# The last feed-forward item of a spectral block: its products in another order, the last comparisons earlier

## The chip, the cores and the metric

One Trainium2 chip, one of its cores. The metric is the device time of one execution in microseconds (us); of several executions the median counts. A profile is one further execution, recorded with every instruction's begin and end.

## The reference

`x` has 2048 rows of 512. It goes through a Fourier mixing of rows and columns and then through a gated feed-forward block of inner width 1792; both sit behind a normalization with a learned shift, scale and gate.

```python
x = A_x
mod = (_silu(c) @ w_mod).reshape(c.shape[0], 6, 1, -1)
sa, ca, ga, sb, cb, gb = (mod[:, 0], mod[:, 1], mod[:, 2], mod[:, 3], mod[:, 4], mod[:, 5])
h = _layernorm(x, axis=-1) * (1 + ca) + sa
x = x + ga * _A_ref(h, A_dft_seq_re, A_dft_seq_im, A_dft_hid_re, A_dft_hid_im)
h = _layernorm(x, axis=-1) * (1 + cb) + sb
x = x + gb * _B_ref(h, B_w1, B_w3, B_w2)
```

`_A_ref` multiplies by the real and imaginary DFT matrices that are given as inputs. `_B_ref` is `(silu(h @ w1) * (h @ w3)) @ w2`.

## The kernel before, in words

`folded` computes the Fourier part with about half of the products, since DFT matrices are symmetric. Whether the given matrices are so, it finds out itself: it loads them a second time in pieces (tiles `cx`, `cy`, `cz`, `cv`; `cx` and `cz` by queue SP, `cy` and `cv` row by row by POOL) and compares the pieces on DVE, counting differences in `cnt`. `judge` (L1759) sums the counts in a chain of some twenty small DVE instructions down to one flag, `bad`. Behind the last store every engine loads the flag, and if it is set, the program goes on with `general`, a second version without the shortcut. The comparisons are a queue of work beside the products: `to_load` holds loads, `checks` holds comparisons, and `look` (L2649), called after each unit of products, starts loads while more than `spare()` of the 50 SBUF slots are free, and starts a comparison once its tiles were begun `LAG` = 9 units ago.

The feed-forward block runs over 14 items: 2 pairs of row blocks (a pair is two blocks of 512 rows) by 7 groups of 256 inner columns. Each item is made of units of six matmuls of 128x512 (two contraction halves by three passes, since every factor is split into a high and a low part of fp32):

- a1 to a7 are the products with `w1`, b1 to b7 those with `w3`. Seven products give what eight would, in the way of Winograd: the four results (two halves of the group's columns by two row blocks) are sums of products. The products 1, 6, 7, 4 add up in one PSUM bank (bank 0 for a, 3 for b), 2 has a bank of its own (1 or 4), and 5 and 3 share one (2 or 5). Between them `factor` (L2100) takes partial sums out: ACT copies (`x`, `y`), DVE adds (`plus`).
- A result of a goes through SiLU on ACT; the matching result of b is multiplied to it on DVE; then the high part of the product is made on ACT and the low part on DVE (both in a tile `hf`). `behind(n, ...)` puts a step behind the n-th following unit.
- Of the four results, two belong to the first row block: they need the products 1, 2, 6, 7, 4. The two of the second row block need 5 and 3 too.
- y units are the products of `hf` with `w2`. An item has eight: four blocks of 128 output columns for the first row block and four for the second. They are put into the queue `seconds` once the item's results are on the way, and run between the units of the next item. For the last two items a y unit's sum is multiplied by the gate and added to `xr` on DVE (L1890); the last item's are then stored by queues SP and ACT (L1861).

The order of units is written by hand as a string for each item (`head + body`, L2767 on); "-b7" is a unit of the item before, "y" the next of `seconds`, "J" runs what is left of the comparisons and then `judge`. In this text y1 to y8 are the eight y units of the last but one item, and z1 to z8 those of the last item (z1 to z4 for its first row block).

The y units take PSUM banks 6 and 7 in turn. In the last item, once all seven a products are issued, the list becomes five banks long:

```python
if not more and kind == "a" and state[i, "w1"]["n"] == 7:
    down_banks[:] = [6, 7, 0, 1, 2]
```

A unit of the same list place waits until the sum that was there has been read.

Of the kernel before, what the change touches and what calls it, by code (L numbers as in the profile page):

```python
# [43 lines left out]
def folded(nc, pools, c, cp, wmr, wmc, x, xt, ctr, cti, wdr, wdi, w1, w3, w2, out):  # L44
# [42 lines left out]
    def copy(dst, src, scale=1.0):  # L87
        nc.scalar.activation(dst, src, AF.Copy, scale=scale)  # L88
# [1549 lines left out]
    to_load = deque()  # L1638
# [278 lines left out]
    def weight_jobs(i, w):  # L1917
        key = (w, *items[i])
        use = wuse[key] = {}

        def highs():
            use["h"] = take(F32R, w + "h")
            copy(flat(use["h"]), flat(wraw[key]))

        def totals(engine="DVE"):
            use["s"] = take(F32, w + "s")
            s, r = four(use["s"]), four(wraw[key])
            tensors(engine, s[:, 0, :], r[:, 2, :], r[:, 3, :], OP.add)
            tensors(engine, s[:, 1, :], s[:, 0, :], r[:, 0, :], OP.subtract)
            tensors(engine, s[:, 2, :], r[:, 0, :], r[:, 2, :], OP.subtract)  # L1930
            tensors(engine, s[:, 3, :], r[:, 1, :], s[:, 1, :], OP.subtract)

        def lows(engine="DVE"):
            use["l"] = take(F32R, w + "l")
            r = wraw.pop(key)
            tensors(engine, flat(use["l"]), flat(r), flat(use["h"]).bitcast(F32), OP.subtract)
            give(r)

        def sum_highs():
            use["sh"] = take(F32R, w + "sh")  # L1940
            copy(flat(use["sh"]), flat(use["s"]))

        def sum_lows(engine="DVE"):
            use["sl"] = take(F32R, w + "sl")
            tensors(engine, flat(use["sl"]), flat(use["s"]), flat(use["sh"]).bitcast(F32), OP.subtract)
            give(use.pop("s"))
            done.add(("ready", i, w))

        step(jobs, 1, highs, 0.0, 1.0)
        step(jobs, 1, totals, 1.4)  # L1950
        step(jobs, 1, lows, 1.2)
        step(jobs, 1, sum_highs, 0.0, 1.0)
        step(jobs, 1, sum_lows, 1.2)
# [145 lines left out]

    def factor(i, w, n):  # L2100
        g, pair = items[i]
        key = (w, g, pair)
        st = state.setdefault((i, w), {})
        new = n in (1, 2, 5)
        if new:
            st[TO[n]] = bank(TO[n] + (0 if w == "w1" else 3))
        to = st[TO[n]]
        names = ("h", "l") if LEFT[n][0] == "h" else ("sh", "sl")
        for d in range(2):
            at = slice(int(LEFT[n][1]) * HALF + d * P, int(LEFT[n][1]) * HALF + (d + 1) * P)  # L2110
            product(
                to,
                [flat(wuse[key][x])[:, at] for x in names],
                [x[:, d, :] for x in right(pair, n)],
                new and d == 0,
                d == 1,
                not new,
            )
        if n == 1:
            st["x"] = take(F32, "x")  # L2120
            if w == "w1":
                vs[i] = [take(F32, "v") for _ in range(2)]
        if n == 5:
            st["y"] = take(F32, "x")
        if n in (1, 5, 6):
            copy(st["y" if n == 5 else "x"][:, n // 6, :], to)
        elif n == 4:
            result(i, w, 1, 0, to)
        else:

            own = st["y" if n == 7 else "x"][:, n % 2 if n < 7 else 0, :]
            q, k = {2: (0, 0), 3: (0, 1), 7: (1, 1)}[n]
            dst = vs[i][q][:, k, :] if w == "w1" else own
            plus(dst, to, own)
            result(i, w, q, k, dst)
            if n == 7:
                behind(1, lambda: give(st["y"]))
        st["n"] = st.get("n", 0) + 1
        if st["n"] == 7:
            for x in wuse.pop(key).values():  # L2140
                give(x)
        if n == 3:
            behind(1, lambda: give(st["x"]))
            if w == "w3":
                for x in vs.pop(i):
                    behind(9 if items[i] in SEVEN else 3, lambda x=x: give(x))
# [494 lines left out]


    LAG, AHEAD, SPARE = 9, 7, 7
    clock, begun_at, paused = [0], {}, []

    def spare():
        return SPARE if ("xc", NT - 1) in done else SPARE + 2

    def look(force=False):  # L2649
        clock[0] += 1  # L2650
        while to_load and not paused and (len(free) > spare() or force) and len(begun_at) < AHEAD:
            key, fn = to_load.popleft()
            begun_at[key] = clock[0]
            fn()
        while checks:
            tiles, cost, fn = checks[0]
            late = any(x not in begun_at or clock[0] - begun_at[x] < LAG for x in tiles)
            if not force and (late or jobs or credit[0] <= 0):
                return
            if any(x not in begun_at for x in tiles):  # L2660
                return
            checks.popleft()
            credit[0] -= cost
            fn()
            for x in [x for x in begun_at if x not in cq]:
                begun_at.pop(x)
# [13 lines left out]
    turning = NG  # L2680
# [10 lines left out]
    def early_w3(i):  # L2691
        return items[i][1] == 1

    def unit(kind, i, n):
        g, pair = items[i]
        more = i + 1 < len(items)
        if n == 1:
            drain(lambda: ("ready", i, "w1" if kind == "a" else "w3") in done, jobs)
        if (kind, i, n) == ("a", turning, 1):
            drain(lambda: not background, background)  # L2700
        if kind == "a" and i == turning and n in (4, 5, 6, 7):
            drain(lambda: ("t", 1, {6: 2, 5: 1, 7: 3, 4: 4}[n]) in done, jobs)
        delayed()
        factor(i, "w1" if kind == "a" else "w3", n)
        if (kind, n) == ("a", 1):
            load_w(("w1", *items[i + 1]) if more else ("w2", g, pair))
        if (kind, n) == ("a", 6):
            load_w(("w2", g, pair))
        if not more and kind == "a" and state[i, "w1"]["n"] == 7:
            down_banks[:] = [6, 7, 0, 1, 2]  # L2710
        if (kind, n) == ("a", 7 if i == turning else 3) and more:
            load_w(("w3", *items[i + 1]))
            weight_jobs(i + 1, "w1")
        if (kind, n) == ("b", 2):
            (seven_jobs if (g, pair) in SEVEN else plain_jobs)(("w2", g, pair))
        if (kind, n) == ("b", 3):
            if i + 2 == turning:
                for at in ((PAIRS[1][0], 0), (PAIRS[1][0], 1), (PAIRS[1][1], 1)):
                    chunk_parts(background, *at, 3)
                sums_of.append(pair_sums(1))  # L2720
            if i + 1 == turning:
                other_operands()
            if more and not early_w3(i):
                weight_jobs(i + 1, "w3")
            if (g, pair) in SEVEN:
                seconds.extend((g, pair, n, ("w2", g, pair)) for n in ORDER7)
            else:
                for t in PAIRS[pair]:
                    seconds.extend((g, pair, t, d, ("w2", g, pair)) for d in range(ND))
        if (kind, n) == ("b", 6) and more and early_w3(i):  # L2730
            weight_jobs(i + 1, "w3")
        beside(1.36, FACTOR[kind][n])

    operand = {1: "h2l{0}.0", 2: "h2l{0}.1", 3: "h2l{1}.1", 5: "tl1", 6: "tl2", 7: "tl3", 4: "tl4"}
    prev = [f"all{b}.{m}" for b in (2, 3) for m in range(2)]
# [28 lines left out]
    for i in range(len(items)):  # L2764

        paused[:] = [i] if turning - 1 <= i < turning else []
        body = "a6 a5 y y a7 y a3 y a4 y b1 y b2 y b6 b5 y"  # L2767
        if i == turning:
            body = "y y y y y a6 y a5 y a7 y b1 b2 a4 b6 a3 b5"
        if i == len(items) - 1:  # L2770
            body = "a6 y a5 y b1 a7 y a3 b2 a4 y b6 b5 y b7 J y b4 b3 " + "y " * 10
        head = "-b7 a1 a2 -b4 -b3 "
        for what in (head + body).split() if i else []:
            if what == "J":
                while checks:
                    look(True)
                judge()
            elif what == "y":
                if not seconds:
                    continue  # L2780
                if (i, len(seconds)) == (len(items) - 1, 4):
                    tc.mark_branch_hint_location("general", hint="LikelyTaken")
                down(*seconds.popleft())
            elif what[0] == "-":
                unit(what[1], i - 1, int(what[2]))
            else:
                unit(what[0], i, int(what[1]))
# [806 lines left out]
```

## Time and profile before

| | |
|---|---|
| median of 3 runs | 638.33 us (637.39 to 640.04) |
| profiled execution | 641.07 us |
| its span, first to last instruction | 639.3 us |
| PE busy | 607.3 us, 95% of the span |
| DVE busy | 514.1 us, 80% |
| ACT busy | 391.0 us, 61% |
| POOL busy | 215.2 us, 34% |
| mean granted PE clock | 0.982 of full speed |

A row of the timeline gives start, busy time, engine, line, operation and tiles (out<-in) and, in brackets, how long the engine had been idle and who released it. Matmuls are pipelined: a row lasts 0.39 us, but the next starts 0.23 us after it. PEclk, the granted clock, is 1.00 where PE runs at full speed. Times count from the span's start.

### The profile page before, as it was taken

To read this page: it belongs to the slowest core of one execution; us is meant where nothing else is said; L and a number is where in the kernel's file an instruction comes from. 1 tells how busy PE (TensorE), PEld (TensorE's weight loads), DVE (VectorE), ACT (ScalarE), POOL (GpSimd) and SP (SyncE) were. 2 spreads that over 40 slices of the span, in tenths; PEclk is the share of its full clock that TensorE was granted. 3 is DMA by queue.
4 is the path that set the end of the run, shared out by engine and by line. 5 is a ranking of instruction groups with operands and counts; after the bars stand their busy time and mean duration, and the time that the engine had idled before them with its cause. 6 is when DMAs were issued, how large, how long until landed. Compare 5 with 4: busy or idle time off the path is not lost.

```text
span 639.3 us, 8734 instructions
## 1 busy us (share of the span) xinstructions
PE 607.3 (95%) x2893; PEld 491.5 (77%) x2893; DVE 514.1 (80%) x1017; ACT 391.0 (61%) x626; POOL 215.2 (34%) x234
## 2 busy tenths in 40 slices
PE   8998899999969999989999999899999999999984
PEld 3778889767747888868877888687878888888864
DVE  4997879889986998468947797699888979879883
ACT  2587787527665557976875666485656556665310
POOL 7344114483951022103023321510553344434000
PEclk9999999999969999999999999899999999999998
DMA  7762345798143398738679967999999999999406
GB/s 243 220 192 71 100 110 155 224 249 226 66 157 107 91 204 207 131 103 172 137 151 262 269 173 149 239 190 195 261 285 258 260 229 261 238 253 269 145 1 136
DMA packets 61585, 118.11 MB, mean 185 GB/s; under 512 B 10649, under 2 KB 29081, under 8 KB 61532
## 3 DMA queue, kind: packets, MB, share of 16 engines
q1 hardware_dynamic: 45068, 67.66, 38.3%
q0 software_dynamic: 13536, 46.93, 33.3%
q10 hardware_dynamic: 2928, 2.88, 1.6%
q8 instruction: 24, 0.39, 0.3%
q14 instruction: 29, 0.24, 0.1%
HBM read 84.94 MB, written 35.65 MB: 189 GB/s over the span
## 4 chain that ended last, share of the span: by engine, by line
PE 71%; DVE 11%; issue 8%; DMA 5%; ACT 3%; POOL 1%; DVEq 0%; ACTq 0%; POOLq 0%
PE banks L106 53%; PE banks L1295 4%; DMA sum<-y 3%; PE banks L929 3%; PE banks L1325 2%; DVE w3s L100 2%; PE banks L1474 2%; PE banks L599 1%; DMA wmr<-in_wmr 1%; PE banks L948 1%; PE banks L827 1%; PE banks L729 1%; DVE w1s L100 1%; DVE x L94 1%; DVE ml L100 1%
## 5 line engine op out<-in xcount | busy, mean ns | idle before, releaser
L106 PE MATMUL banks<-hf,w2h 128*128 128x512 f32 (+1 forms) x452 | 141.5, 393 | 6.2 <-DVE hf L91 3.1
L1899 POOL DMA_DIRECT2D sum<-y x48 | 44.7, 931 | 244.5 <-ACT y L656 206.4
L106 PEld LDWEIGHTS banks<-hf,w2h 128*128 128x128 f32 x452 | 84.9, 189 | 26.4 <-DVE hf L91 5.0
L106 PE MATMUL banks<-hf,w2l 128*128 128x512 f32 (+1 forms) x226 | 88.1, 390 | 0.0
L656 ACT ACTIVATE y<-banks,gb 128x512 f32<-128x512 f32 x96 | 65.5, 683 | 27.3 <-PE banks L106 24.0
L88 ACT ACTIVATE hf<-v 128x512 fp32r<-128x512 f32 x56 | 35.3, 631 | 62.4 <-DVE v L97 53.5
L94 DVE TENSOR_TENSOR x<-banks,x 128x512 f32<-128x512 f32 x42 | 28.9, 689 | 43.2 <-PE banks L106 40.4
L88 ACT ACTIVATE x<-banks 128x512 f32<-128x512 f32 x84 | 48.8, 591 | 18.2 <-PE banks L106 16.5
L1983 ACT ACTIVATE v<-v 128x512 f32<-128x512 f32 x42 | 26.5, 632 | 39.7 <-DVE v L94 38.9
L106 PEld LDWEIGHTS banks<-hf,w2l 128*128 128x128 f32 x226 | 42.9, 190 | 8.7
L94 DVE TENSOR_TENSOR v<-banks,x 128x512 f32<-128x512 f32 x42 | 28.9, 688 | 19.4 <-PE banks L106 19.0
L91 DVE TENSOR_TENSOR hf<-v,hf 128x512 fp32r<-128x512 f32 x56 | 38.4, 686 | 4.0 <-ACT hf L88 3.7
L106 PE MATMUL banks<-th,w3sh 128*128 128x512 f32 x84 | 33.2, 395 | 0.3 <-ACT x L88 0.3
L106 PE MATMUL banks<-th,w1sh 128*128 128x512 f32 x84 | 32.9, 392 | 0.0
L106 PE MATMUL banks<-tl,w1sh 128*128 128x512 f32 x84 | 32.8, 390 | 0.0
L106 PE MATMUL banks<-th,w3sl 128*128 128x512 f32 x84 | 32.7, 390 | 0.0
L106 PE MATMUL banks<-th,w1sl 128*128 128x512 f32 x84 | 32.7, 390 | 0.0
L106 PE MATMUL banks<-tl,w3sh 128*128 128x512 f32 x84 | 32.7, 389 | 0.0
L599 PE MATMUL banks<-tmp 128*128 128x128 f32 (+1 forms) x140 | 27.9, 350 | 3.1 <-DVE tmp L489 3.1
L97 DVE TENSOR_TENSOR v<-v,x 128x512 f32<-128x512 f32 x42 | 29.2, 695 | 1.4
L599 PEld LDWEIGHTS banks<-tmp 128*128 128x128 f32 x140 | 19.6, 199 | 11.5 <-issue 8.4
L1295 PE MATMUL banks<-us,mh 128*128 128x512 f32 x64 | 25.9, 404 | 0.0
(361 smaller groups left out, 1694.3 us busy)
## 6 DMA issues: line engine op xcount, KB each, us to landing
sum<-y POOLq DMA_DIRECT2D x48, 512.0 KB
w<-in_w SPq DMA_DIRECT2D x42, 512.0 KB
wmc<-in_wmc SPq DMA_DIRECT2D x8, 512.0 KB
cx<-in_ctr SPq DMA_DIRECT2D x16, 256.0 KB
cz<-in_ctr SPq DMA_DIRECT2D x16, 256.0 KB
cx<-in_cti SPq DMA_DIRECT2D x16, 256.0 KB
cz<-in_cti SPq DMA_DIRECT2D x16, 256.0 KB
sum<-xm SPq DMA_DIRECT2D x8, 512.0 KB
```

The costliest lines, as they stand in the source:

```text
L88: nc.scalar.activation(dst, src, AF.Copy, scale=scale)
L91: nc.vector.tensor_tensor(out=dst, in0=a, in1=b, op=OP.subtract)
L94: nc.vector.tensor_tensor(out=dst, in0=a, in1=b, op=OP.add)
L97: nc.vector.tensor_tensor(out=dst, in0=a, in1=b, op=OP.mult)
L100: (nc.gpsimd if engine == "POOL" else nc.vector).tensor_tensor(out=dst, in0=a, in1=b, op=op)
L106: nc.tensor.matmul(acc, lhs[a], rhs[b], start=first and n == 0, stop=last and n == len(PASSES) - 1, skip_group_check=more,)
L599: nc.tensor.matmul(warm[:, :width], onesf[:, :P], onesf[:, :width], start=True, stop=True)
L656: nc.scalar.activation(dst, src, AF.Identity, scale=by)
L929: nc.tensor.matmul(halves(hb[k])[:, m, :], sides((hh, hl)[a][k])[:, dt, m, :], wu[dt][:, b, m, :], start=False, stop=dt % 2 == 1 and n == ...
L1295: nc.tensor.matmul(acc(b, m), (mh, ml)[p][b, o][:, m, cols(a)], (us, ul)[q][k][:, m, :], start=(o, a, n) == (0, 0, 0), stop=False, skip_gr ...
L1899: nc.gpsimd.dma_start(sums[t, d // 2], y, accum_op=OP.add)
L1983: behind(k != 0 or q == 0, lambda: nc.scalar.activation(v, src, AF.Silu))
```

## The change

Only the last item's string, and what hangs on it, changes. Its products for the first row block (1, 2, 6, 7, 4) come first, for `w1` and `w3`, and 5 and 3 later; the y units of its first row block may thus begin before b3.

```diff
-            body = "a6 y a5 y b1 a7 y a3 b2 a4 y b6 b5 y b7 J y b4 b3 " + "y " * 10
+            ending.append(i)
+            body = "a6 y b1 a7 y b2 a4 y b6 y b7 y b4 y a5 y J a3 y b5 y b3 " + "y " * 7
```

Since 7 now precedes 5, `factor` copies the sum of the products 1, 6, 7 into `y` and adds 5 to it; before, it copied 5 and added the sum. For the last item:

```diff
+        kept, added = (7, 5) if split_blocks(i) else (5, 7)
...
-        if n == 5:
+        if n == kept:
             st["y"] = take(F32, "x")
-        if n in (1, 5, 6):
-            copy(st["y" if n == 5 else "x"][:, n // 6, :], to)
+        if n == kept:
+            copy(st["y"][:, 0, :], to)
+        elif n in (1, 6):
+            copy(st["x"][:, n // 6, :], to)
...
+    def split_blocks(i):
+        return i == len(items) - 1
...
+        if (kind, n) == ("b", 4 if split_blocks(i) else 3):
             if (g, pair) in SEVEN:
```

The last lines queue the item's own y units already at b4. For the comparisons, two numbers change at the end: `spare()` is 4 in the last item, so that the last loads begin sooner, and once nothing is left to load a comparison may start 7 units after its tiles instead of 9.

```diff
     def spare():
+        if ending:
+            return 4
         return SPARE if ("xc", NT - 1) in done else SPARE + 2
...
-            late = any(x not in begun_at or clock[0] - begun_at[x] < LAG for x in tiles)
+            late = any(x not in begun_at or clock[0] - begun_at[x] < (LAG if to_load else 7) for x in tiles)
```

How the instructions move on their engines is shown at three places. On PE, ahead of z1. Before, z1 (tiles `hf_694` and `hf_697` with `w2h_692`) follows y7 and y8 (`hf_687`, `hf_681`), and these follow b3:

```order
L106 MATMUL banks_71<-hf_687_5307,w2h_668_5198 128x512 x2
L106 MATMUL banks_71<-hf_687_5307,w2l_672_5213 128x512
L106 MATMUL banks_71<-hf_681_5264,w2h_668_5198 128x512 x2
L106 MATMUL banks_71<-hf_681_5264,w2l_672_5213 128x512
L106 MATMUL banks_71<-hf_694_5396,w2h_692_5392 128x512 x2
L106 MATMUL banks_71<-hf_694_5396,w2l_693_5394 128x512
L106 MATMUL banks_71<-hf_697_5494,w2h_692_5392 128x512 [waits Activation_49]
L106 MATMUL banks_71<-hf_697_5494,w2h_692_5392 128x512 [waits DVE_49]
```

Now y8 (`hf_688`, `hf_682`) follows a3 (`h2h_437` with `w1sh_662`), then come b5 and z1:

```order
L106 MATMUL banks_71<-h2l_439_3600,w1sh_662_5143 128x512
L106 MATMUL banks_71<-h2h_437_3590,w1sl_663_5152 128x512
L106 MATMUL banks_71<-hf_688_5310,w2h_668_5198 128x512 [waits DVE_49]
L106 MATMUL banks_71<-hf_688_5310,w2h_668_5198 128x512
L106 MATMUL banks_71<-hf_688_5310,w2l_672_5213 128x512
L106 MATMUL banks_71<-hf_682_5267,w2h_668_5198 128x512 x2
L106 MATMUL banks_71<-hf_682_5267,w2l_672_5213 128x512
L106 MATMUL banks_71<-th_462_3773,w3sh_677_5240 128x512
```

The first product of y8 has got a wait for DVE; the one in z1's second half went. On DVE, behind the last instruction of J (`bad`). Before, a y unit's `xr`, then the work for b7, b4 and b3 follows:

```order
L1795 TENSOR_SCALAR bad_244<-fine_5470 1x1 [waits DVE_49]
L1890 SCALAR_TENSOR_TENSOR xr_678_5250<-banks_71,gb_233,xr_678_5250 128x512 [waits PE_49]
L91 TENSOR_TENSOR hf_696_5477<-v_684_5274,hf_696_5477 128x512 [waits Activation_49]
L97 TENSOR_TENSOR v_684_5274<-v_684_5274,banks_71 128x512 [waits PE_49]
L94 TENSOR_TENSOR x_691_5357<-banks_71,x_691_5357 128x512 [waits PE_49]
```

Now a3's addition (into `v_684`), y8's `xr`, b5's addition (`x_695`) and what hangs on it:

```order
L1795 TENSOR_SCALAR bad_244<-fine_5478 1x1 [waits DVE_49]
L94 TENSOR_TENSOR v_684_5276<-banks_71,x_683_5275 128x512 [waits PE_49]
L1890 SCALAR_TENSOR_TENSOR xr_679_5251<-banks_71,gb_233,xr_679_5251 128x512 [waits PE_49]
L94 TENSOR_TENSOR x_695_5412<-banks_71,x_695_5412 128x512 [waits PE_49]
L97 TENSOR_TENSOR v_685_5277<-v_685_5277,x_695_5412 128x512 [waits DVE_49,Activation_49]
```

So a3's addition stands behind J. On queue SP, the last loads. Before, the last `w2` precedes the two pieces of the last `cz`:

```order
L1848 DMA xr_678_5250<-sum_3_0_3140 128x1024 [waits DMAHW0_49,DMASW3_49,DVE_49]
L1848 DMA xr_679_5251<-sum_3_1_3172 128x1024 [waits DMAHW1_49,DMAHW3_49,DMASW6_49,DVE_49]
L1804 DMA w2_685_5276<-in_w2 128x1024 [waits DMAHW2_49]
L289 DMA cz_689_5334<-in_cti 64x2x512 [waits PE_49]
L289 DMA cz_689_5334<-in_cti 64x2x512 [waits DMAHW4_49]
```

Now it follows them:

```order
L1848 DMA xr_678_5250<-sum_3_0_3140 128x1024 [waits DMAHW0_49,DMASW3_49,DVE_49]
L1848 DMA xr_679_5251<-sum_3_1_3172 128x1024 [waits DMAHW1_49,DMAHW3_49,DMASW6_49,DVE_49]
L289 DMA cz_681_5264<-in_cti 64x2x512 [waits DMAHW2_49,PE_49]
L289 DMA cz_681_5264<-in_cti 64x2x512
L1804 DMA w2_686_5279<-in_w2 128x1024 [waits DMAHW4_49,DVE_49]
```

The two programs hold equally many products, additions, copies, loads and stores.

More of the change, by code (lines that the diff above doesn't have):

```diff
@@ L2129, in factor @@
         else:
-            own = st["y" if n == 7 else "x"][:, n % 2 if n < 7 else 0, :]
-            q, k = {2: (0, 0), 3: (0, 1), 7: (1, 1)}[n]
+            own = st["y"][:, 0, :] if n == added else st["x"][:, n % 2, :]
+            q, k = {2: (0, 0), 3: (0, 1), added: (1, 1)}[n]
             dst = vs[i][q][:, k, :] if w == "w1" else own
@@ L2135, in factor @@
             result(i, w, q, k, dst)
-            if n == 7:
+            if n == added:
                 behind(1, lambda: give(st["y"]))
@@ L2643, in folded @@
     LAG, AHEAD, SPARE = 9, 7, 7
+    ending = []
     clock, begun_at, paused = [0], {}, []
     def spare():
+        if ending:
+            return 4
         return SPARE if ("xc", NT - 1) in done else SPARE + 2
@@ L2710, in unit @@
             down_banks[:] = [6, 7, 0, 1, 2]
-        if (kind, n) == ("a", 7 if i == turning else 3) and more:
+        if (kind, n) == ("a", 7 if i == turning else 5 if split_blocks(i) else 3) and more:
             load_w(("w3", *items[i + 1]))
@@ L2731, in unit @@
             weight_jobs(i + 1, "w3")
-        beside(1.36, FACTOR[kind][n])
+        beside(1.36, FACTOR[kind][12 - n if split_blocks(i) and n in (5, 7) else n])
     operand = {1: "h2l{0}.0", 2: "h2l{0}.1", 3: "h2l{1}.1", 5: "tl1", 6: "tl2", 7: "tl3", 4: "tl4"}
```

## The prediction

> **What bounds the kernel now.** I read the chain of waits first, for the last 80 us only, because the change touches nothing earlier; then the TensorE (PE) timeline there; then VectorE (DVE). Unit names (a, b, y, z, J) are those of the part on the kernel; start and busy time stand at a row's head.
>
> ```profile
> 559.84 49.11 PE banks L106 x216
> ...
> 616.98 0.66 DVE xr L1890
> ...
> 620.82 10.33 PE banks L106 x50
> ```
>
> And two stretches of five microseconds (after the limits and the length: busy time of PE, of its weight loads, of DVE, ACT and POOL, then the granted clock):
>
> ```profile
> 610.00:615.00 5.00, 4.91 (x22) 3.76 (x21) 4.82 (x22) 0.63 (x1) 0.00 (x0) 1.00 0.01 2
> 615.00:620.00 5.00, 3.61 (x15) 2.46 (x14) 4.66 (x17) 0.63 (x1) 0.00 (x0) 1.00 0.00 0
> ```
>
> PE carries the end up to 609 and again from 620.8; between them the chain is DVE's. The two stretches say the same: from 615 to 620 PE is busy for 3.61 of 5 us while DVE has 4.66. The gap on PE, row by row:
>
> ```profile
> 589.60 0.39 PE L106 MATMUL banks<-th,w1sh 128*128 128x512 f32 x1
> ...
> 591.64 0.73 PE L106 MATMUL banks<-hf,w2h 128*128 128x512 f32 x2
> ...
> 617.32 0.62 PE L106 MATMUL banks<-hf,w2h 128*128 128x512 f32 x2
> 617.78 0.39 PE L106 MATMUL banks<-hf,w2l 128*128 128x512 f32 x1
> 619.55 0.50 PE L106 MATMUL banks<-hf,w2h 128*128 128x512 f32 x1 [1.39 <-ACT hf L88]
> 620.82 0.50 PE L106 MATMUL banks<-hf,w2h 128*128 128x512 f32 x1 [0.77 <-DVE hf L91]
> ...
> 621.38 0.62 PE L106 MATMUL banks<-hf,w2h 128*128 128x512 f32 x2
> ...
> 622.74 0.62 PE L106 MATMUL banks<-hf,w2h 128*128 128x512 f32 x2
> ...
> 630.86 0.28 PE L106 MATMUL banks<-hf,w2l 128*128 128x256 f32 x1
> ```
>
> Units follow each other every 1.36 us (621.38 to 622.74). The last item's a6 starts at 589.60 and is unit 0; z1 is unit 20 and would start at 589.60 + 20 x 1.36 = 616.80. It starts at 617.32, 0.52 late; 0.13 of that is at 591.64 (0.73 instead of 0.62 and the step behind it), ahead of everything that moves. z1 then takes 621.38 - 617.32 = 4.06 instead of 1.36, since its second half waits for `hf` of b4, which DVE delivers late. **2.70 + 0.52 = 3.22 us are lost; at most 3.09 can come back.** From 621.38 on nothing is lost.
>
> **The change, part by part.** Both programs hold the same products, additions and stores; only places differ, so there is no term for work. In the new order unit k starts at 589.73 + 1.36k if nothing waits.
>
> *Gained.* Six units (8.2 us) now lie between b4 and z1. For the `hf` of b4's result ScalarE (ACT) and DVE need, by the page's groups:
>
> ```profile
> L88 ACT ACTIVATE hf<-v 128x512 fp32r<-128x512 f32 x56 | 35.3, 631 | 62.4 <-DVE v L97 53.5
> L91 DVE TENSOR_TENSOR hf<-v,hf 128x512 fp32r<-128x512 f32 x56 | 38.4, 686 | 4.0 <-ACT hf L88 3.7
> ```
>
> 0.63 and 0.69 us fit in with much to spare: the 2.70 go. The comparisons that stood right ahead of J are now spread over five units ahead of it; they lie beside PE's work, and without that cover they cost at most what they take ahead of J now, about 2 us (609.64 to 613.07 in the rows below, less two additions of 0.69). The rest of the 0.52 (b4 behind a DVE addition) goes too. Gain: 3.09.
>
> *A new wait.* y8 is unit 17 and stands right behind a3. Since a3 is the last of the w1 products, the list of banks becomes [6, 7, 0, 1, 2] there, and the running count puts y8 at its fifth place: bank 2, where a3's sum lies. That sum is read by DVE (`plus`, row `v_684 <- banks, x_683` in the order), and this addition stands behind the whole of J. DVE's times for it, from the old tail:
>
> ```profile
> 607.42 0.62 PE L106 MATMUL banks<-hf,w2h 128*128 128x512 f32 x2
> 608.98 0.75 DVE L1890 SCALAR_TENSOR_TENSOR xr<-banks,gb,xr 128x512 f32<-128x512 f32 x1 [1.81 <-PE banks L106]
> 609.64 0.21 DVE L1708 SCALAR_TENSOR_TENSOR cv<-cv,cl 128x32 f32<-128x32 f32 x1
> ...
> 611.01 0.69 DVE L94 TENSOR_TENSOR x<-banks,x 128x512 f32<-128x512 f32 x1
> ...
> 613.07 0.63 DVE L1762 TENSOR_SCALAR cnt<-cnt,mask 128x8 f32<-128x8 f32 x4
> ...
> 616.91 0.73 DVE L1890 SCALAR_TENSOR_TENSOR xr<-banks,gb,xr 128x512 f32<-128x512 f32 x1
> ...
> 620.08 0.68 DVE L91 TENSOR_TENSOR hf<-v,hf 128x512 fp32r<-128x512 f32 x1
> ```
>
> A unit's result reaches DVE 1.56 after the unit starts (607.42 to 608.98). y7, unit 15, starts at 610.13, so its `xr` begins at 611.69; the next instruction, J, follows 0.66 later (608.98 to 609.64) at 612.35. J lasts 3.84 (613.07 to 616.91): 616.19. The addition takes 0.69: 616.88; PE follows 0.06 later (620.08 + 0.68 to 620.82): **y8 starts at 616.94 instead of 589.73 + 17 x 1.36 = 612.85, 4.09 late.** Behind y8 on PE stand b5, z1, b3 and all else; everything waits.
>
> What is late next: b3 adds into the bank that b5's addition on DVE must first read. With y8 at 616.94, b5 ends and its result is there at 618.30 + 1.56 = 619.86, read by 620.55; b3 starts at 621.02. Nothing more. z5, the first that needs b3's result, comes three units behind b3's end: 4.1 us for a sum, a product and two `hf` pieces, 2.7 us, and one `xr` between them.
>
> Sum on PE: 4.09 + 0.13 - 3.22 = **+1.00 us**. The tail behind the last product stays:
>
> ```profile
> 631.17 0.48 DVE L1890 SCALAR_TENSOR_TENSOR xr<-banks,gb,xr 128x256 f32<-128x256 f32 x1 [0.23 <-PE banks L106]
> ```
>
> From here to the end of the span at 639.3 are 8.1 us of store, flag and branch. The stores keep their order and the last one hangs on the last product alone, so I take these over unchanged.
>
> *The clock.* A gap of about 4 us on PE may cost more than its length. The old timeline of PE around a gap of 2.34 us:
>
> ```profile
> 187.10 0.79 PE L106 MATMUL banks<-h2h,w1h 128*128 128x512 f32 x1
> ...
> 404.45 0.39 PE L106 MATMUL banks<-hf,w2h 128*128 128x512 f32 x1
> 407.18 0.50 PE L106 MATMUL banks<-hf,w2h 128*128 128x512 f32 x1 [2.34 <-DVE hf L91]
> ...
> 407.75 1.06 PE L106 MATMUL banks<-hf,w2h 128*128 128x512 f32 x2
> 408.60 0.63 PE L106 MATMUL banks<-hf,w2l 128*128 128x512 f32 x1
> ```
>
> And four stretches with their clock, the last one behind PE's last product:
>
> ```profile
> 407.00:408.00 1.00, 0.82 (x3) 0.74 (x4) 1.00 (x2) 0.01 (x1) 0.94 (x1) 0.87 1.10 276
> 411.00:412.00 1.00, 1.00 (x5) 0.78 (x5) 0.26 (x1) 0.24 (x1) 0.46 (x1) 0.93 1.07 283
> 192.50:193.00 0.50, 0.50 (x4) 0.41 (x3) 0.30 (x1) 0.00 (x0) 0.00 (x0) 0.81 0.00 0
> 633.00:633.25 0.25, 0.00 (x0) 0.00 (x0) 0.00 (x0) 0.00 (x0) 0.00 (x0) 0.52 1.03 295
> ```
>
> 0.87 over 407 to 408 puts the drop to a half at 407.74; 0.93 puts the return at 411.14: 3.4 us at half clock after a 2.34 us gap. At the end it drops at 633.0, 1.9 us after PE's last row. After another gap, dense work begins at 187.10 and the clock returns at 192.69 (0.81 over its half microsecond): 5.6 us. A gap of 4 us is longer than 2.34 and 1.9, so I expect a drop. At half clock a matmul takes 0.85 / 2 = 0.425 (407.75 to 408.60) instead of 1.36 / 6 = 0.227: 0.47 of the time is lost. 3.4 us cost 1.6, 5.6 us cost 2.6; bounds for the cost are 0 (no drop) and 3.2 (6.8 us, twice the shortest). I take 4.5 us, between the two cases with dense work: **+2.1 us**.
>
> From 407.74 to 633.01 are 66 steps of 3.413 us, from 192.69 to 407.74 are 63, from 407.74 to 411.14 is one. The clock seems to be judged in fixed stretches, and in this execution one ended at 633.01 - 4 x 3.413 = 619.36, between the old gap's two pieces (618.2 to 619.55 and 620.05 to 620.82). With another phase both fall into one stretch, 2.2 us idle of 3.4, about as much as at 404 to 407, and the old kernel pays 1.6 there too; that is about half of the phases, **-0.8 us** on the median.
>
> The Trainium skill, "TensorE: Matmul & The Clock Gate", section "What's actually happening", gives a free-running window of 3413 ns, which this trace's steps agree with. It also says that the clock falls after at least one idle window of about 3.4 us. By that rule the new gap, 3.9 us from the end of a3's last product to 616.94, would halve the clock only where a whole window falls into it, by my estimate in about 15% of the phases, and else the sum would be +1.0. The row of 2.34 us disagrees.
>
> **Sum.** In this execution's own terms 641.07 + 1.00 + 2.1 = 644.2. The shown runs have their median at 638.33, 2.74 below it; to it I add 1.00 + 2.1 - 0.8 = 2.3: **640.6 us**.
>
> **The rivals.**
>
> *The clock holds.* The gap is there, but stretches that it fills only partly don't count. For it: the gaps of 1.39 and 0.77 us did no harm here. Against: 2.34 did. 638.33 + 1.0 = 639.3. It is what the page's rule gives in most phases.
>
> *The weights come late, slower.* In the new order SyncE (SP) issues the two pieces of the last `cz` ahead of the last `w2`:
>
> ```profile
> 593.22 0.42 SPq L1804 DMA_DIRECT2D w<-in_w x1
> 593.69 1.90 SPq L289 DMA_DIRECT2D cz<-in_cti x2
> 600.00:601.00 1.00, 1.00 (x6) 0.84 (x5) 0.39 (x2) 0.00 (x0) 0.00 (x0) 1.00 0.03 10
> 602.08 1.04 ACT L88 ACTIVATE w2h<-w 128x1024 fp32r<-128x1024 f32 x1
> ```
>
> `w2` leaves at about 595.2, 2 us later, while ACT comes to it at 596, behind a7's copy, 6 us sooner than now. The copy of `w2` stands ahead of b6's copy, for which b7 (unit 10, 603.33) waits. Two further ACT rows:
>
> ```profile
> L88 ACT ACTIVATE x<-banks 128x512 f32<-128x512 f32 x84 | 48.8, 591 | 18.2 <-PE banks L106 16.5
> ...
> L1983 ACT ACTIVATE v<-v 128x512 f32<-128x512 f32 x42 | 26.5, 632 | 39.7 <-DVE v L94 38.9
> ```
>
> From the arrival on: `w2h` 1.04, an `hf` 0.63, a SiLU 0.63, b6's copy 0.59, in all 2.9; so an arrival behind 600.4 costs its delay. The transfers are over by 600 (share 0.03), so I take 0; but the old use at 602.08 only bounds the landing from above, and 602 would cost 1.6: 642.2.
>
> *The bank is not the one waited for, faster.* If y8 wrote elsewhere it would run at 612.85, and b3 (unit 20, 616.93) would be the first to wait: behind J come 0.69 + 0.66 + 0.69 for a3's addition, y8's `xr` and b5's addition and the 0.06, so b3 starts at 618.29. 1.36 + 0.13 - 3.22 = -1.7 and no drop: 636.6. The point is J's end: before about 614.8 b3 wouldn't wait either, -3.1, 635.2. The program names DVE in the wait of y8's first product, which speaks against it.
>
> **How the numbers follow.** Forecast 0.62, clock holds 0.15, weights late 0.12, faster 0.08, else 0.03. The range reaches from the case without a clock drop, less 1.3 for the scatter of runs, 638.0, to the forecast with 6.8 us at half clock and no credit from the old gap, 638.33 + 1.0 + 3.2 = 642.5, and half a microsecond of late weights: 643.0. 0.5% is 3.2 us, about what a measurement of this kernel can tell from no change. Above 641.5 lie a quarter of the forecast, most of the late weights and some of the rest: 0.26. Below 635.1 only the end of the faster case: 0.04. The rest 0.70.
>
> **What would show it.** A single gap of about 4 us ahead of y8, released by DVE's addition after the last row of J; no gap ahead of z1 or its second half; granted clock 0.5 for 3 to 7 us from then on; the last product 1 us later than now plus the clock's cost. I am wrong if PE runs through y8, if b7 waits for ACT, or if the clock stays at 1.00.

## The result and the profile after

| | before | after |
|---|---|---|
| median | 640.16 us (20 runs, 637.39 to 642.3) | 644.6 us (20 runs, 640.03 to 647.64) |
| ratio | | 1.0068, 95% interval 1.005 to 1.0087 |
| profiled execution, its span | 641.07, 639.3 us | 645.09, 643.2 us |
| from a6's first product to the last product | 41.26 us | 45.41 us |
| from there to the end of the span | 8.44 us | 7.90 us |

The changed kernel is slower by 4.4 us (3.2 to 5.6), where 2.3 were forecast. The fourth row is the cleanest measure: both programs are the same ahead of a6, and yet a6 starts anywhere from 586.6 to 591.1 in the profiled executions of this study. From a6 on the change costs 4.15 us, and nothing behind the last product.

PE's timeline of the changed kernel (start, busy time, engine, line, tiles; in brackets the idle time and who ended it) holds two stops, and no longer the two in z1:

```profile
589.89 0.39 PE L106 MATMUL banks<-th,w1sh 128*128 128x512 f32 x1
...
604.90 0.50 PE L106 MATMUL banks<-th,w3sh 128*128 128x512 f32 x1 [1.10 <-ACT x L88]
...
613.19 0.49 PE L106 MATMUL banks<-h2h,w1sh 128*128 128x512 f32 x1
...
618.63 0.73 PE L106 MATMUL banks<-hf,w2h 128*128 128x512 f32 x2 [3.78 <-DVE v L94]
...
635.30 0.28 PE L106 MATMUL banks<-hf,w2l 128*128 128x256 f32 x1
```

The second stop is y8 behind a3, and DVE's timeline of the same kernel shows what it waits for:

```profile
613.39 0.75 DVE L1890 SCALAR_TENSOR_TENSOR xr<-banks,gb,xr 128x512 f32<-128x512 f32 x1 [0.27 <-PE banks L106]
614.06 0.62 DVE L1762 TENSOR_SCALAR cnt<-cnt,mask 128x8 f32<-128x8 f32 x4
617.84 0.14 DVE L1795 TENSOR_SCALAR bad<-fine 1x1 int32<-1x1 f32 x1
617.91 0.67 DVE L94 TENSOR_TENSOR v<-banks,x 128x512 f32<-128x512 f32 x1
```

J runs from 614.06 to 617.91 (3.85 us), then the addition that reads a3's sum, then y8 at 618.63. A row ends 0.16 after the next product could start, so y8 was due at 618.63 - 3.78 - 0.16 = 614.69 and is 3.94 late.

The first stop is b7, due at 589.89 + 0.13 + 10 x 1.36 = 603.62 and 1.28 late. Two views tell why, the timelines of SP and of ACT in the changed kernel:

```profile
594.20 1.25 SPq L289 DMA_DIRECT2D cz<-in_cti  x2
595.54 0.55 SPq L1804 DMA_DIRECT2D w<-in_w  x1
```

```profile
602.29 1.06 ACT L88 ACTIVATE w2h<-w 128x1024 fp32r<-128x1024 f32 x1 [6.02 <-DMA w<-in_w]
603.26 0.61 ACT L88 ACTIVATE hf<-v 128x512 fp32r<-128x512 f32 x1
603.78 0.58 ACT L1983 ACTIVATE v<-banks 128x512 f32<-128x512 f32 x1
604.26 0.59 ACT L88 ACTIVATE x<-banks 128x512 f32<-128x512 f32 x1
```

The last `w2` leaves behind `cz`, ACT stands for 6.02 us until it has landed, and b6's copy (604.26), for which b7 waits, is the third behind it. The clock, in windows of one microsecond (limits, length, busy time of PE, its loads, DVE, ACT and POOL, then the granted clock, the DMA share and GB/s):

```profile
617.00:618.00 1.00, 0.00 (x0) 0.00 (x0) 0.83 (x8) 0.00 (x0) 0.00 (x0) 1.00 0.00 0
...
619.00:620.00 1.00, 1.00 (x6) 0.82 (x5) 0.00 (x0) 0.24 (x1) 0.00 (x0) 1.00 0.00 0
620.00:621.00 1.00, 1.00 (x5) 0.77 (x4) 0.67 (x1) 0.00 (x0) 0.00 (x0) 0.58 0.00 0
...
623.00:624.00 1.00, 1.00 (x5) 0.75 (x4) 0.90 (x2) 0.00 (x0) 0.00 (x0) 0.71 0.00 0
```

It halves at 620.16 (0.58) and is back at 623.58 (0.71): 3.42 us at half speed, which cost 0.47 x 3.42 = 1.6. The sum for this execution: the stretch from a6 would last 41.26 - 3.22 = 38.04 without any loss; 1.28 for b7, 3.94 for y8 and 1.6 for the clock make 44.86, and 0.55 of the measured 45.41 is left: 0.13 of it is the delay right behind a6 that both kernels have, and the rest is probably the slower first products behind each stop (0.50 instead of 0.39 at b7).

### The profile page after: what moved, and what is told of

Read it like the earlier page. It is cut to its first block, busy times and chain, and to the rows that moved or that the text cites. A ratio compares the mean times of both kernels' runs of the same rounds, so it can differ in the third digit from the quotient of the medians.

```text
span 643.2 us, 8735 instructions
## 1 busy us (share of the span) xinstructions
PE 609.3 (95%) x2893; PEld 493.4 (77%) x2893; DVE 515.8 (80%) x1017; ACT 391.2 (61%) x626; POOL 216.2 (34%) x234
## 4 chain that ended last, share of the span: by engine, by line
PE 75%; DVE 12%; DMA 4%; ACT 4%; issue 3%; POOL 1%; SPq 1%; DVEq 0%; ACTq 0%; POOLq 0%
PE banks L106 57%; PE banks L1295 4%; PE banks L599 3%; PE banks L1325 2%; DMA w<-in_w 2%; DVE w3s L100 2%; PE banks L929 2%; PE banks L1474 2%; DMA sum<-y 1%; PE banks L827 1%; PE banks L948 1%; PE banks L729 1%; DVE w1s L100 1%; DVE ml L100 1%; SPq L1853 1%
```

## The experiments

Each kernel was run beside the kernel before on the same chip; the ratio is to that. "Clock" is the median over the runs of the mean granted clock of an execution; 0.001 of it is 0.64 us of full speed. The last two columns are from one profiled execution each: the stretch from a6 to the last product, and the stops in it with their idle time in brackets of the timeline.

| kernel | ratio (95%) | clock | a6 to last | stops |
|---|---|---|---|---|
| before | 1 | 0.984 | 41.26 | z1: 1.39, 0.77 |
| changed | 1.0068 (1.005 to 1.0087) | 0.981 | 45.41 | b7 1.10, y8 3.78 |
| changed, again | 1.0056 (1.0026 to 1.0086) | 0.981 | 45.17 | y8 3.83 |
| e1: other bank | 0.9972 (0.995 to 0.9994) | 0.985 | 41.91 | b7 2.00, b3 1.01 |
| e2: w2 first | 1.0031 (1.0016 to 1.0046) | 0.981 | 45.03 | y8 3.91 |
| e3: both | 0.9939 (0.9917 to 0.9962) | 0.988 | 39.58 | b3 1.10 |
| e3, again | 0.9967 (0.995 to 0.9984) | 0.986 | 39.59 | b3 1.10 |
| e4: idle products | 1.0032 (1.0003 to 1.0061) | 0.984 | 43.20 | b7 0.50, y8 0.21 |
| e5: w2 first, idle products | 0.9996 (0.9973 to 1.0019) | 0.984 | 42.42 | y8 0.28 |
| e6: before, idle products | 1.0007 (0.999 to 1.0023) | 0.984 | 41.29 | z1 0.40 |
| e7: both, J later | 0.9964 (0.9945 to 0.9984) | 0.983 | 38.17 | none |
| e7, again | 0.999 (0.9964 to 1.0015) | 0.9825 | 38.22 | none |
| e8: J later alone | 1.0021 (0.9996 to 1.0046) | 0.9825 | 39.44 | y8 0.78 |

**The changed kernel once more.**

> The changed kernel once more, so that the others of this job stand beside it on one chip. Expected ratio to the kernel before 1.0068 (1.005 to 1.009), that is about 4.4 us; a b7 gap of 0.5 to 2 us, a y8 gap of about 3.9 us. By the runs' mean granted clock (which each run lists) the changed kernel spent about 24.6 us' worth at half clock and the kernel before 20.8; that difference of 3 to 4 us, times 0.47, is the clock's part, 1.4 to 1.9 us. A rival (waits alone, no clock) expects equal mean clocks in both.

The ratio came again, within the expected range. But its profiled execution has no stop at b7 at all: `w2` was issued 4.50 us after a6's start (5.65 in the first) and its copy began 11.05 after a6 (12.40). And the clock cost more there; its windows:

```profile
617.00:618.00 1.00, 0.00 (x0) 0.00 (x0) 0.86 (x7) 0.00 (x0) 0.00 (x0) 0.77 0.00 0
618.00:619.00 1.00, 0.51 (x1) 0.50 (x2) 0.43 (x1) 0.53 (x1) 0.00 (x0) 0.50 0.00 0
...
624.00:625.00 1.00, 1.00 (x5) 0.78 (x5) 0.88 (x2) 0.00 (x0) 0.00 (x0) 0.82 0.00 0
```

The drop is at 617.54, still inside the gap, the return at 624.36: 6.82 us, of which 5.87 lie behind y8's start at 618.49 and cost 2.8. So the two lesser costs (b7's wait and the clock) change places from one execution to the next, at nearly the same total (45.41 and 45.17). Over the runs the mean clock is 0.003 below that of the kernel before, some 1.9 us.

**e1: y8 in another bank.** The fourth and fifth of the list change places, so that y8 writes bank 1, which was read long ago.

```diff
-            down_banks[:] = [6, 7, 0, 1, 2]
+            down_banks[:] = [6, 7, 0, 2, 1]
```

> The changed kernel with the list of banks as [6, 7, 0, 2, 1]: y8 writes bank 1 instead of bank 2. Theory (y8 waits for DVE's reading of a3's sum in bank 2): the gap of 3.9 us ahead of y8 goes, b3 waits about 1.2 us for b5's addition instead, no drop of the clock; 4.0 to 5.0 us faster than the changed kernel, within 1 us of the kernel before. Rival (PE waits for DVE to get through J whatever the bank): the gap stays within 0.5 us of 3.9, time as the changed kernel.

The gap at y8 is gone and the next wait is that of b3, by 1.01. PE's timeline in this kernel:

```profile
604.41 0.50 PE L106 MATMUL banks<-th,w3sh 128*128 128x512 f32 x1 [2.00 <-ACT x L88]
...
619.43 0.50 PE L106 MATMUL banks<-h2h,w3sh 128*128 128x512 f32 x1 [1.01 <-DVE x L94]
```

The clock stays at 1.00 from 560 on to the last product. By the ratios the edit gives back 5.4 to 6.1 us of the changed kernel, more than expected, and the kernel lies 1.8 below the kernel before where within 1 was expected; by the profiled stretch it gives back only 3.3 to 3.5, in an execution where b7 stood longest of all (2.00). The bank is the cause of the larger part, and the two numbers say how well its size is known.

**e2: w2 ahead of cz.** The last `w2` is asked for before `spare()` falls to 4 and lets `cz` through.

```diff
+            load_w(("w2", *items[i]))
             ending.append(i)
```

> The changed kernel with the last w2 load issued ahead of the last cz load again. Theory (w2 is late because it stands behind cz in SP's queue): ACT's copy of w2 starts before 600.5, no gap ahead of b7, 1.0 to 1.6 us faster than the changed kernel, 2.5 to 3.5 slower than the kernel before. Rival (the transfers are late by contention, whatever their order): w2 still lands at 601.5 or later and the gap of 1.1 us ahead of b7 stays; time as the changed kernel.

ACT's copy of `w2` now starts 9.27 us after a6, b7 does not wait, and the ratio falls by 0.0025 to 0.0037, 1.6 to 2.4 us: somewhat more than the 1.0 to 1.6 expected, though the intervals of the two kernels overlap. The traces are clearer. In all six profiled executions with `w2` first (e2, e3 and e7 twice each, e5) the copy starts 8.4 to 10.1 us after a6 and b7 never waits; with `cz` first it starts 11.05 to 13.32 after a6, and b7 waits in three of five. In the profiled execution the gap at y8 stayed and took the long form of the clock:

```profile
615.00:616.00 1.00, 0.00 (x0) 0.00 (x0) 0.93 (x5) 0.00 (x0) 0.00 (x0) 0.51 0.00 0
616.00:617.00 1.00, 0.79 (x2) 0.70 (x3) 0.15 (x1) 0.63 (x1) 0.00 (x0) 0.50 0.00 0
...
621.00:622.00 1.00, 1.00 (x4) 0.76 (x3) 0.27 (x1) 0.00 (x0) 0.00 (x0) 0.58 0.00 0
```

It is half speed from 615.02 to 621.84, 6.82 us again. The clock's cost does not hang on the late `w2`.

**e3: both.** The two edits together.

> Both edits. Theory: the two gaps go together, b3's wait of 1.2 us for b5's addition is the only one left; 5.5 to 6.5 us faster than the changed kernel, 1 to 2.5 us faster than the kernel before. Rival (one of the two is hidden behind the other): no faster than the better one of the two single edits.

> Both edits once more (bank list [6, 7, 0, 2, 1], w2 ahead of cz), beside the late J on one chip. 0.9939 again (0.992 to 0.996); mean granted clock of the runs 0.985 to 0.987, where the kernel before has 0.984; 7.5 us from the start of the last addition to the end of the span.

The end of the chain of waits in the first of the two (start, length, engine, tile, line) goes through y7's `xr`, J and the three additions behind it to b3, and no longer through y8:

```profile
608.68 0.75 DVE xr L1890
...
613.13 0.14 DVE bad L1795
613.27 0.60 DVE v L94
613.87 0.66 DVE xr L1890
614.53 0.61 DVE x L94
615.14 0.04 issue
615.18 11.28 PE banks L106 x54
```

Both measurements are below the kernel before, by 3.9 and 2.1 us; this order with another bank and another place for `w2` is faster than both kernels of the study. The size is known less well than the sign: the first gain is more than was expected, and the second ratio, 0.9967, lies above its expected range. By the stretch and the tail behind it the two executions agree (39.58 and 7.84, 39.59 and 7.79): 2.3 us less than the kernel before. The tail from the start of the last addition is 7.5 us in both, as expected.

**e4: idle products in the gap.** Sixteen products that nobody uses, into bank 1, stand between a3 and y8 and keep PE busy while y8 waits. They take 16 x 0.227 = 3.6 us, less than the gap.

```diff
-... y J a3 y b5 y b3 "
+... y J a3 F y b5 y b3 "
...
+            elif what == "F":
+                for _ in range(16):
+                    nc.tensor.matmul(bank(1), u[:, 0, cols(0)], v[:, 0, :], start=True, stop=True)
```

> The changed kernel with 16 idle matmuls (3.6 us, into a bank that is free then) between a3 and y8, so that PE is busy while it waits. Theory (the gap also costs 1.6 us or more through the halved clock): the clock stays at 1.00 behind the gap, y8 starts when it did, 1.2 to 2.5 us faster than the changed kernel. Rival (only the wait itself costs): no difference of more than 0.5 us.

y8 still waits for the same addition, but the clock does not move; windows of five microseconds:

```profile
615.00:620.00 5.00, 4.79 (x22) 3.64 (x21) 2.52 (x11) 0.63 (x1) 0.00 (x0) 1.00 0.00 0
620.00:625.00 5.00, 5.00 (x24) 4.15 (x23) 4.70 (x8) 1.27 (x2) 0.00 (x0) 1.00 0.17 52
```

The ratio falls by 0.0024 to 0.0036 (1.5 to 2.3 us), the mean clock rises from 0.981 to 0.984. The intervals of the two overlap, so the median alone would not settle it. In the traces y8 meets the same wait, no drop follows, and the stretch, less b7's delay (0.68 here, 1.28 and 0 in the changed kernel), is 42.52 where the changed kernel has 44.13 and 45.17: 1.6 and 2.65 us less, as much as was worked out for the clock there (1.6 and 2.8). More work on PE made this part of the kernel faster; the cost of the clock is shown, and 1.5 to 2.3 us is its size on the median.

**e5: w2 first, and idle products.** What is left is y8's wait alone.

> w2 loaded ahead of cz, and 16 products without use (into bank 1) between a3 and y8. What is left is y8's wait for its bank alone, without the clock and without the late w2. Theory (waits and clock add up): against w2 alone (ratio 1.0031) about 2 us less, since the gap of 3.9 us no longer halves the clock; against both edits (ratio 0.9939) y8's 4.1 us less b3's 1.1 us, about 2.9 us more; both give 638.5 to 639.5 where the kernel before has 640, ratio 0.997 to 0.9995, and the granted clock stays at 1.00 in the tail. Rival (what w2 alone has left is not the clock but the wait): 1.002 to 1.004, as without the idle products.

The stretch is 42.42, 2.84 above e3's 39.58 (2.9 expected), 2.61 below e2's 45.03 (5.63 us at half clock behind y8's start in e2 are worth 2.65). The ratio, 0.9996, is just above what was expected and 0.0035 (2.2 us) below e2's; their intervals just overlap. In the traces the three costs add up.

**e6: does the old gap cost clock too?** Nine idle products stand ahead of z1 in the kernel before, in z1's own bank.

```diff
-... y b4 b3 " + "y " * 10
+... y b4 b3 " + "y y F " + "y " * 8
```

> The kernel before, with 9 products without use ahead of z1, in the bank that z1 is about to fill; they last 2.04 us, less than the 2.2 us that z1 loses there anyway. Theory (the old gap halves the clock too, in some or most runs): faster than the kernel before by 0.8 us (the prediction's credit) to 2.1 us, ratio 0.9967 to 0.9988, and the mean granted clock higher by 0.001 to 0.003. Rival (the old gap costs its length alone, as the profiled execution showed): ratio 1.000 +- 0.001, equal mean clock.

The rival was right: 1.0007, the same mean clock of 0.984, and the stretch from a6 is 41.29 against 41.26. No cost of the clock shows for the old gap of 1.39 and 0.77 us. By the interval's lower end, 0.999, filling it brought at most 0.6 us: the credit of 0.8 us on the median is not there, a smaller one is not excluded.

**e7: J behind z3.** Both edits of e3, and J later, so that nothing on PE waits for it.

```diff
-... y a5 y J a3 y b5 y b3 " + "y " * 7
+... y a5 y a3 y b5 y b3 y y J " + "y " * 5
```

> Both edits (bank list [6, 7, 0, 2, 1], w2 ahead of cz) and J moved from before a3 to behind z3, so that DVE reads a3's and b5's sums, and b3 its bank, ahead of J. Theory (b3's 1.1 us is DVE's J, and nothing else is late): no PE gap over 0.5 us, the last product 1.1 us sooner than with both edits, ratio 0.991 to 0.9925 (both edits: 0.9939). Rival (J now stands ahead of the last y units' additions on DVE or the flag is late): a bank wait or a longer tail behind the last product, ratio 0.994 to 0.998.

> Both edits and the late J once more. Theory (the last product comes 0.8 us sooner than with both edits, but J keeps DVE until 623.4, six additions follow back to back, their stores bunch, and the tail is 1.8 us longer): 0.5 to 1.5 us slower than both edits, ratio 0.995 to 0.998; 9 us or more from the start of the last addition to the end of the span. Rival (the difference of the two was chance of the clock's phase): equal within 0.3 us, tail 7.5 us.

PE does not stop once, and the stretch is 38.17 and 38.22, which is the loss-free 38.04 and the 0.13. Yet the kernel is slower than e3 by about 1.5 us both times (0.0025 and 0.0023 of the ratio, within overlapping intervals): the rival with the longer tail, not the 0.991 to 0.9925 of the theory. The second ratio, 0.999, is above its expected range, the difference from e3 within it. DVE's timeline in the first run:

```profile
623.34 0.14 DVE L1795 TENSOR_SCALAR bad<-fine 1x1 int32<-1x1 f32 x1
623.41 3.48 DVE L1890 SCALAR_TENSOR_TENSOR xr<-banks,gb,xr 128x512 f32<-128x512 f32 x6
```

The last six additions wait for J and follow each other without a pause, and so do their stores. From the last product to the end of the span it takes 10.43 and 10.18 us, where e3 takes 7.84 and 7.79. By the issues of the DMA view in the last 14 to 16 us a store of queue SP lands after 4.6 us at the median, in e3 after 3.7:

```profile
out<-xr SPq DMA_DIRECT2D x6, 128.0 KB, 4.6
```

```profile
out<-xr SPq DMA_DIRECT2D x6, 128.0 KB, 3.7
```

The mean clock of its runs is lower as well (0.983 and 0.9825, e3 0.988 and 0.986). PE's idle tail counts in that mean, and longer tails lower it without a cost. Stretch and tail together are 48.60 and 48.40 us, in e3 47.42 and 47.38: the longer tail, less what PE gained, explains 1.0 to 1.2 of the 1.5 us.

**e8: J later alone.** The changed kernel with its own bank list and its own place for `w2`.

> The changed kernel with J alone moved from before a3 to behind z3; list of banks [6, 7, 0, 1, 2] and place of w2's load as in the change. Theory (y8 waits 3.9 us because the addition that reads its bank stands behind J): the bank is still that of a3's sum, so y8 still waits for DVE, but for a3's result (1.56 from a3's start, less the 1.36 that a3 lasts) and one addition (0.69) and 0.06 alone: a gap of about 0.95 us ahead of y8, released by DVE's v at L94. The late w2 stays (b7 0.5 to 2 us), and the tail behind the last product is 1.8 us longer, as in the run with both edits and a late J (there 9.3 us from the start of the last addition to the end of the span, where both edits alone have 7.5). Sum: that run's 0.9964 and 2.2 to 2.8 us more, ratio 0.9998 to 1.0008, 3 to 4 us faster than the changed kernel. Rival (the wait is for something else, e.g. the comparisons of J or the copy on ACT): a y8 gap of 3 to 4 us as before.

y8 still waits for DVE's `v`, but for 0.78 instead of 3.8:

```profile
611.20 0.73 PE L106 MATMUL banks<-hf,w2h 128*128 128x512 f32 x2 [0.78 <-DVE v L94]
```

So the long wait needs both, the bank and J: with another bank it is gone (e1), with J out of the way 0.78 of it is left. The ratio, 1.0021, is above the expected range, its interval (from 0.9996) reaches into it; the tail was 10.66 us. By its trace (39.44 and 10.66) the kernel would be 0.4 us above the kernel before (41.26 and 8.44), which is in the expected range.

## Why the prediction was right and wrong

**The place and the mechanism were right.** There is one long gap, ahead of y8, released by DVE's addition behind J; 4.09 late was forecast, 3.94 measured. The 2.70 at z1's second half went, and nothing new waits between y8 and the end. e3 and e7 confirm the arithmetic: the rival in which y8 meets a free bank gave 1.36 + 0.13 - 3.22 = -1.7 for the stretch, and e3's is 39.58 - 41.26 = -1.68; no wait at all gave -3.1, and e7's is -3.09.

**The clock was right, and sized well.** 4.5 us at half speed, 2.1 us, were taken; the profiled executions have 3.42, 5.87 and 5.63 behind y8's start (1.6, 2.8, 2.6), and e4 puts the cost at 1.5 to 2.3 on the median. That the size came out is in part luck. The 4.5 lay between two cases, and the longer one, 5.6, was counted from 187.10, though by the rows PE was at work from 182.18; and no case here has 4.5, but either one step of 3.41 or two, less what falls into the gap. The rival in which the clock holds fell: the y8 gaps of the three unfilled profiles (the two of the changed kernel and e2) all have the drop. The two drops inside the gap took 6.82 us, twice the 3.413 that the traces step by. The Trainium skill, "TensorE: Matmul & The Clock Gate", section "What's actually happening", names a window of 3413 ns: the step agrees. Its condition for a drop, a whole idle window, does not. The step that ended at 620.16 began at 616.75, and PE was at work in it from 618.63, 45% of it; yet the clock fell.

A share of work does not sort the steps sharply either. In the step before that one, 613.33 to 616.75, PE was at work until 614.85, also 45%, and the clock held (the row of 617 to 618 has 1.00). In all thirteen profiled executions, with the steps laid by each one's own changes of clock and the work taken from PE's busy time, every step at full clock with 42% or less, behind the first 10 us, was followed by half clock, and every one with 52% or more by full clock; between these, at 44 to 50%, both came. The gap of 2.34 us that the prediction used stands in all thirteen: it halved the clock in eleven, and in e1 and e3 (first) not, where a step's end cuts it so that PE was at work 47% of the step with the larger part. A gap of 3.8 us puts at least 1.9 us of idle time into one step of 3.413, wherever a step ends, and so leaves that step at about 45% or less; the changed kernel's first profile has it cut almost in half, and there it cost one step.

**The step that failed is the late `w2`, taken as 0.** The condition was nearly right: "an arrival behind 600.4 costs its delay", 10.8 us after a6; in the profiles it is about 11.1: an ACT copy that starts 11.05 or 11.08 after a6 stops nobody, and at 11.80, 12.40 and 13.32 (e4, changed, e1) b7 is 0.68, 1.28 and 2.18 behind its due time. The landing was wrong. `w2` was said to leave at about 595.2, and left at 595.54; from there it took 6.75 us until ACT could start, and 6.35 to 7.45 in the other four executions with this order. (With `w2` first it took 4.61 to 7.18, from an earlier start in most of them.) The prediction read in the old trace "The transfers are over by 600 (share 0.03)"; in the changed kernel the end of the traffic itself is later (the last two numbers are the DMA share and GB/s):

```profile
600.00:601.00 1.00, 1.00 (x6) 0.83 (x5) 0.22 (x1) 0.00 (x0) 0.00 (x0) 1.00 0.61 207
601.00:602.00 1.00, 1.00 (x6) 0.84 (x5) 0.00 (x0) 0.00 (x0) 0.00 (x0) 1.00 0.12 37
```

The prediction's own rival (1.6, chance 0.12) describes what happened, and b7 waiting for ACT was among its own signs of being wrong. The measured size: b7 is 0 to 2.2 us late in the five profiled executions with this order, 0.8 in the mean; moving `w2` brought 1.6 to 2.4 in the runs (e2), 2.3 from e4 to e5, and 0.3 to 2.1 from e1 to e3.

**The credit of -0.8 was wrong.** It rested on a step's end that was said to spare the old gap in half of the phases only. e6 shows no gain from filling that gap, and leaves room for 0.6 us at most. By the shares above, the gap's 2.1 us of idle time would have to lie almost whole (1.8 to 2.0) in one step, which is less than half of the phases.

**The base was low.** The sum in the terms of the profiled execution was 644.2, close to the measured median of 644.6, but by luck: that execution, 641.07, lies 0.9 above the median of twenty, and the sum has nothing for `w2`. It was then lowered by 2.74 to the median of the three runs shown, 638.33. Twenty runs have 640.16, and 1.8 us of the miss are this sample; the credit makes 0.8 and `w2` 0.8 to 1.6 of the 4.0 between 640.6 and 644.6. Put together: 1.00 for the waits, 0.8 (the mean of five profiles) to 1.6 for `w2` and about 2.1 for the clock are 3.9 to 4.7; measured were 4.4, and 3.6 the second time.

What stays open: from a6's first product to the last the profiled executions explain themselves to about half a microsecond, but a6 itself starts up to 4.5 us apart in the same code. A part of that is the clock: between 20 us and a6 the traces hold three whole steps at half speed (e3's first, a6 at 586.58) to six (changed, again, a6 at 591.10). It is not all, since with five a6 starts at 586.80 in e8 and at 589.89 in the changed kernel. Differences below some 2 us between two kernels in the table, such as e1 against e3, rest on that scatter as much as on the edit.

## What to carry to other kernels

When an order is changed, write down for every bank or buffer that is used again who reads it last, and what stands ahead of that reader on its own engine; here a chain of some twenty tiny instructions stood there, and another bank took the wait away. A load that is used earlier and issued later must be timed to its landing behind everything that is under way, not to the end of the traffic in the old trace. A gap on PE can cost more than its length (here 3.8 us did; for the old 1.39 and 0.77 no such cost showed), and a few products without use tell how much more.

## What the hardware showed that was not expected

Sixteen products that nobody needs made the kernel 1.5 to 2.3 us faster by the medians, and kept the clock at 1.00 in the traces. A gap of 3.8 to 3.9 us cost between 1.6 and 2.8 us of clock beyond its length, by where it fell against the 3.413 us steps: one step at half speed in one execution, two in two others, where a step with PE at work 65% (e2, from 615.02) or 72% (changed, again, from 617.53) did not yet bring the clock back. No wholly idle step was needed for a drop: 42% of work and less never saved the clock, 52% and more always did (before: 65%, idle from about 618.2 to 619.36 of a step that began at 615.95), and 45% went both ways within a single execution (changed). And one transfer of 512 KB took 6.35 to 7.45 us from its issue to its use behind other loads, a scatter of a microsecond that goes into the time of the kernel once the transfer is late.
